# Three streamed weight blocks in two portions: 120 partitions over fifteen DMA engines, 8 over eight

## The chip, the core and the metric

The kernel runs on one core of one Trainium2 chip. The metric is the time of one execution on the device in microseconds; lower is better. The runs shown are three of the kernel before, and one further execution was taken with the hardware profiler.

## The reference

Two independent parts are computed, and their results stand side by side in the last dimension of the output (1, 2048, 2048). Part A is attention over segments with a memory that is carried from one to the next. Its cost lies in a chain of 64 segments, each of which needs the one before:

```python
for s in range(n_seg):                       # 64 segments of 32 rows
    xs = x[:, s * seg_len:(s + 1) * seg_len, :]
    h = jnp.concatenate([mem, xs], axis=1)   # 8 memory rows + 32 rows, 1024 wide
    q = jnp.einsum('btd,dhe->bhte', h, Wq)   # Wq, Wk, Wv: 1024 x 32 heads x 128
    k = jnp.einsum('btd,dhe->bhte', h, Wk)
    v = jnp.einsum('btd,dhe->bhte', h, Wv)
    scores = jnp.einsum('bhqe,bhke->bhqk', q, k) * scale
    p = _softmax(jnp.where(mask[None, None], scores, -1000000000.0), axis=-1)
    o = jnp.einsum('bhqk,bhke->bhqe', p, v)
    o = jnp.einsum('bhte,hed->btd', o, Wo)   # Wo: 32 x 128 x 1024
    mem = o[:, :M, :]
    outs.append(o[:, M:, :])
```

Part B is a state-space convolution of 2048 steps over 1024 channels, done by transforms. It isn't touched by the change.

## The kernel before

**Two stages and a loop.** Part B comes first, together with what of part A does not depend on the chain (the projections of the last 8 rows of each segment, `Ahead`). Then `part_a` runs the chain: a loop of 64 rounds (`for s in range(NS)`, line 406), one per segment, and after it a short end with the output of the rows that were put off (lines 639 to 670).

**The weights.** Wq, Wk, Wv and Wo are cut into 64 blocks of 128 partitions x 2048 bf16 values, 512 KB each, 4096 B per partition. A block of Wk, Wq or Wv has the key (matrix, half of the heads, chunk of the 1024 rows), a block of Wo the key ("o", u). Every round needs all 64. Most of them stay in SBUF for the whole loop, two whole blocks and two halves are kept in other places (`KEPT`, `HALF`), and twelve do not fit: `STREAM` and `STREAM_O` list them, and they are read from DRAM again in every round. In the order of their use within a round these are k02, q02, k11, k15, q14, v02, v07, v14, v17, o4, o8 and o13 (k15 stands for the key ("k", 1, 5) and so on).

**The copies.** The streamed blocks are not read from the inputs but from copies of their own in DRAM. `streamed_copies` (line 63) makes one tile `WD_...` of [128, 2048] for each, with its 128 rows one behind another, and a list of functions, each of which issues one DRAM-to-DRAM transfer on SP's queue (line 69). Part B calls them one at a time between its own work (line 1273).

**The loads.** In the loop `unit(key)` (line 300) hands out a block. For a streamed one it calls `stage` (line 337), which takes the next of four slots (`SLOTS = 4`, tags w0 to w3 of the tile `wst`) in turn and issues one transfer of 128 partitions from the copy, on SP's queue (line 340):

```python
    def stage(key, in_):
        t_ = wst.tile([128, 2048], BF16, name="wst", tag="w%d" % (loads[0] % SLOTS))
        loads[0] += 1
        nc.sync.dma_start(out=..., in_=in_)
        return t_
```

SP issues its transfers in order. Each waits until TensorE has read the block that was in the slot, four blocks earlier, and until the transfers that used this slot and this semaphore before have landed. The first three streamed blocks of the first round are loaded before the loop by `residents` (line 1709). After the loop the three streamed Wo blocks are loaded once more (line 647).

**Other transfers of a round** are issued by ScalarE: the packed left keys `pk` (line 376), the values and rows `vx` (line 382), the store of the left rows (line 392, 128 rows of 512 B) and that of the output rows (line 396, four groups of 32 rows of 512 B).

**The matrix work of a round.** `quads` (line 407) multiplies the 32 rows of the segment with the blocks of one matrix half on TensorE (line 414); its results leave PSUM through ScalarE (line 420). Then come transposes (425), scores (439, 442), the softmax on VectorE and ScalarE, the product with the values (495, 499) and the output projection `oproj` (line 527). Line 627 turns the memory rows back at the end of each round, two transposes, and so marks the rounds in a trace.

Of the kernel before, what the change touches and what calls it, by code (L numbers as in the profile page):

```python
# [10 lines left out]
BF16 = mybir.dt.bfloat16  # L11
# [13 lines left out]

STREAM = {("k", 0): (2,), ("q", 0): (2,), ("k", 1): (1, 5), ("q", 1): (4,), ("v", 0): (2, 7), ("v", 1): (4, 7)}
STREAM_O = (4, 8, 13)

BANK = {("k", 0): "b0", ("q", 0): "b1", ("k", 1): "b2", ("q", 1): "b0", ("v", 0): "b3", ("v", 1): "b2"}
KEPT = {("k", 0, 7): (("K7a", 0, 512), ("K7b", 512, 512), ("K7c", 1024, 512), ("K7d", 1536, 384), (None, 1920, 128)),  # L30
# [28 lines left out]
def streamed_keys():  # L59
    return [key for key in [(m, t, kc) for (m, t), kcs in STREAM.items() for kc in kcs] + [("o", u) for u in STREAM_O]]  # L60


def streamed_copies(ctx, tc, src):
    nc = tc.nc
    dram = ctx.enter_context(tc.tile_pool(name="a_wd", bufs=1, space=bass.MemoryType.DRAM))
    out, copies = {}, []
    for key in streamed_keys():
        t_ = dram.tile([128, 2048], BF16, name="WD_%s" % "_".join(str(i) for i in key))
        copies.append(lambda t_=t_, key=key: nc.sync.dma_start(
            out=t_[:].rearrange("e (h d) -> e h d", h=2) if key[0] == "o" else t_[:], in_=src(key)))  # L70
        out[key] = t_
    return out, copies


class Ahead:
# [3 lines left out]
    def __init__(self, ctx, tc, x, src, seg_len):  # L79
        self.nc, self.tc, self.x, self.src = tc.nc, tc, x, src  # L80
        self.S, self.Dm = x.shape
        self.SL, self.XM = seg_len, 24
        self.XL, self.KC, self.NS = seg_len - 24, self.Dm // 128, self.S // seg_len
        dram = ctx.enter_context(tc.tile_pool(name="a_dram", bufs=1, space=bass.MemoryType.DRAM))
        self.VXd = dram.tile([self.NS + 1, 128, 256 + self.KC * self.XM], BF16, name="VXd")
        self.PKd = dram.tile([self.NS, 128, 512], BF16, name="PKd")
        self.PVd = [dram.tile([self.NS * self.XL, 2048], BF16, name="PVd%d" % t) for t in range(2)]
        self.OLd = dram.tile([self.NS // 8, 128, 8 * 256], BF16, name="OLd")
# [183 lines left out]
def part_a(ctx, tc, x, src, WD, HE, seg_len, out_a, ahead, W_res, rest, places, first):  # L272
    nc = tc.nc
# [26 lines left out]
    def unit(key):  # L300
        if key in rest:

            rest.remove(key)
            load_resident(tc, wres, src, key, W_res, None, places.pop(0)() if places else None)
        if key in W_res:
            return W_res[key]
        if key in KEPT:
            return ahead_of.pop(key) + halves.get(key, [])
        between.pop(key, lambda: None)()
        if key in first:  # L310
            return first.pop(key)
        if key[0] == "v":
            for k_ in rest[0:3 if key[1] == 0 else 1]:
                rest.remove(k_)
                load_resident(tc, wres, src, k_, W_res)
        return stage(key, WD[key][:])

    ctx_l = ctx_w.enter_context(ExitStack())
    pers = ctx_l.enter_context(tc.tile_pool(name="a_pers", bufs=1))
# [14 lines left out]
    def words(out, in_):  # L334
        nc.vector.tensor_scalar(out=out.bitcast(I32), in0=in_.bitcast(I32), scalar1=0, scalar2=None, op0=ALU.bitwise_or)  # L335

    def stage(key, in_):
        t_ = wst.tile([128, 2048], BF16, name="wst", tag="w%d" % (loads[0] % SLOTS))
        loads[0] += 1
        nc.sync.dma_start(out=t_[:].rearrange("e (h d) -> e h d", h=2) if len(in_.shape) == 3 else t_[:], in_=in_)  # L340
        return t_

    def load_kept(key):
# [62 lines left out]
    for s in range(NS):  # L406
# [123 lines left out]
        a = quads("k", 0, (0, 2, 4, 6, 1, 3, 5, 7))  # L530
        k0 = evac(a, "k0")
        a = quads("q", 0, range(0, 6))
# [4 lines left out]
        a = quads("k", 1, range(0, 3))  # L537
# [16 lines left out]
        a = quads("q", 1, range(KC))  # L554
# [3 lines left out]
        a = quads("v", 0, range(0, 3))  # L558
# [34 lines left out]
        a = quads("v", 1, range(0, 5))  # L593
# [46 lines left out]
    wo = {}  # L640
    for u in order:
        if ("o", u) in W_res:
            wo[u] = W_res["o", u]
        else:
            wo[u] = spare.pop(0)
            if ("o", u) in WD:
                nc.sync.dma_start(out=wo[u][:], in_=WD["o", u][:])
            else:
                nc.sync.dma_start(out=wo[u][:].rearrange("e (h d) -> e h d", h=2), in_=src(("o", u)))
    stores(NS - 1, ob)  # L650
# [6 lines left out]
    for b in range(4):  # L657
        pe = [ps_k.tile([128, 512], F32, name="pe", tag="keep%d" % (2 * (b % 2) + n)) for n in range(2)]
        for u in order:
            for hh in range(2):  # L660
                h = 2 * u + hh
                hi = 16 * (h // 16) + 4 * (h % 4) + (h % 16) // 4
# [983 lines left out]
@with_exitstack  # L1646
def kernel(
    ctx: ExitStack,
    tc: tile.TileContext,
    A_x: bass.AP,  # L1650
    A_mem0: bass.AP,
    A_Wq: bass.AP,
    A_Wk: bass.AP,
    A_Wv: bass.AP,
    A_Wo: bass.AP,
    A_seg_len: bass.AP,
    B_u: bass.AP,
    B_A_re: bass.AP,
    B_A_im: bass.AP,
    B_B_re: bass.AP,  # L1660
    B_B_im: bass.AP,
    B_C_re: bass.AP,
    B_C_im: bass.AP,
    B_log_dt: bass.AP,
    B_Dskip: bass.AP,
    out: bass.AP,
):
    seg_len = int(A_seg_len)
    Dm = A_x.shape[2]
    Db = B_u.shape[2]  # L1670
    out_a = out[0, :, 0:Dm]
    out_b = out[0, :, Dm:Dm + Db]
    src = weight_blocks(A_Wq.rearrange("d h e -> d (h e)"), A_Wk.rearrange("d h e -> d (h e)"),
                        A_Wv.rearrange("d h e -> d (h e)"), A_Wo.rearrange("h e d -> (h e) d"))
    WD, copies = streamed_copies(ctx, tc, src)
    ahead = Ahead(ctx, tc, A_x[0], src, seg_len)
    ctx_w = ctx.enter_context(ExitStack())
    W_res, places, first = {}, [], {}
    rest = Keys(RESIDENT)
    rest.ctx = ahead.ctx = ctx_w  # L1680

    def residents(stay, early, uqs, last):
        def put(t_):
            load_resident(tc, None, src, rest.pop(0), W_res, None, t_)
        for _ in range(EARLY[0]):
            load_resident(tc, stay, src, rest.pop(0), W_res)
            yield
        def some(where, tag, n):
            t_ = where.tile([128, n, 2048], BF16, name="W%d" % n, tag=tag)
            return [t_[:, i, :] for i in range(n)]  # L1690
        for t_ in some(stay, "KT1", 2):
            put(t_)
            yield
        for t_ in early:
            put(t_)
            yield
        put(last[0])
        yield
        for t_ in uqs:
            put(t_)  # L1700
            yield
        ahead.wst = ctx_w.enter_context(tc.tile_pool(name="a_wst", bufs=1, side="right"))
        pool = ctx_w.enter_context(tc.tile_pool(name="a_wre0", bufs=1, side="right"))
        for _ in range(EARLY[1]):
            load_resident(tc, pool, src, rest.pop(0), W_res)
            yield
        for i, key in enumerate([("k", 0, 7)] + streamed_keys()[0:SLOTS - 1]):
            first[key] = t_ = ahead.wst.tile([128, 2048], BF16, name="wst", tag="w%d" % i)
            tc.nc.sync.dma_start(out=t_[:], in_=WD[key][:] if key in WD else src(key))
            yield  # L1710
        for i in [c // 2 for c in PAIRS]:
            places.append(lambda i=i: stay.tile([128, 2048], BF16, name="W1", tag="MI%d" % i))
        for i in range(LATE):
            put(places.pop(0)())
            yield
        put(last[1])
        yield

    low = low_blocks(ctx, tc)
    ahead.low = low.pop()  # L1720
    copies += [lambda t_=t_: load_resident(tc, None, src, rest.pop(0), W_res, None, t_) for t_ in low]

    def first_state(m0, xt):
        nc = tc.nc
        consts = constants(tc, ahead)
        hT = next(consts)
        nc.sync.dma_start(out=xt[:].rearrange("p k r -> p (k r)"), in_=ahead.VXd[0, :, 256:])
        nc.sync.dma_start(out=m0, in_=A_mem0[0])
        pm = yield
        for kc in range(8):  # L1730
            nc.tensor.transpose(out=pm[:, kc, :], in_=m0[:, kc * 128:(kc + 1) * 128], identity=ahead.consts[0][0:8, 0:8])
        nc.vector.tensor_copy(out=hT[:, :, ahead.XM:], in_=pm)
        nc.gpsimd.tensor_copy(out=hT[:, :, 0:ahead.XM], in_=xt[:])
        yield
        next(consts)
        yield

    with ExitStack() as ctx_b:
        part_b(ctx_b, tc, B_u[0], B_A_re, B_A_im, B_B_re, B_B_im, B_C_re, B_C_im, B_log_dt, B_Dskip, out_b, ahead, copies, residents, first_state)
    with ExitStack() as ctx_a:  # L1740
        part_a(ctx_a, tc, A_x[0], src, WD, A_Wo.shape[0] * A_Wo.shape[1], seg_len, out_a, ahead, W_res, rest, places, first)
# [35 lines left out]
```

## Time and profile before

| What | us |
|---|---|
| Median of 3 runs | 1962.2 |
| Lowest and highest run | 1956.45 and 1962.97 |
| Span of the profiled execution | 1954.2 |
| TensorE busy in the span | 1810.2 (93%) |
| VectorE busy | 1379.4 (71%) |
| ScalarE busy | 934.7 (48%) |
| GpSimd busy | 443.1 (23%) |
| First and last transpose of line 627 | 649.8 and 1872.3 |

The span goes from the first to the last instruction of the profiled execution; the runs' times include what lies around it. On the page the span is cut into 40 slices of 48.9 us. The loop over the segments begins in the thirteenth of them and ends in the thirty-ninth. Each digit is the busy share of an engine in that slice in tenths. The line of DMA is the mean over the core's 16 DMA engines. In the list of queues q1 is that of SP, q10 that of ScalarE, q0 that of GpSimd, and q8 and q14 carry instructions; the share is the time that their packets took, of 16 engines' span. In the lists of waits a line names who waited and for whom, the sum in us, how often, and the longest.

### The profile page before, as it was taken

Reading aid. Unit: us, or ns where it says so; the run is one execution under the profiler, and the core shown is the slowest. Engines: PE = TensorE matmul, PEld = TensorE weight load, DVE = VectorE, ACT = ScalarE, POOL = GpSimd, SP = SyncE. Lnnn points to the kernel's source line nnn. Section 1 sums busy time; section 2 is a strip of 40 time slices with the busy share of each in tenths; the row PEclk is TensorE's granted clock in tenths of the full one; section 3 lists DMA queues with packets and bytes.
Section 4 is the critical chain, followed back from the end, with each engine's and each line's share of the span. In section 5 each row is a group of like instructions: output and inputs, shape, how many; then the busy total and the mean of one; then the engine's idle time right before and its main releaser. Section 6 shows DMA issues by size and latency. Waiting matters only on the chain.

```text
span 1954.2 us, 74192 instructions
## 1 busy us (share of the span) xinstructions
PE 1810.2 (93%) x31750; PEld 1106.9 (57%) x31788; DVE 1379.4 (71%) x3431; ACT 934.7 (48%) x1670; POOL 443.1 (23%) x855
## 2 busy tenths in 40 slices
PE   8999999887997899999999999999999999998998
PEld 3666666556775555555555555555555555555554
DVE  8599989889994566666676766676766676666650
ACT  8799989851122334344434443444444444444320
POOL 2364545223222111111111111111111111111120
PEclk8999999878998999999999999999999999999999
DMA  7889898867589999999999999999999999999991
GB/s 222 243 232 283 237 287 243 221 188 253 169 272 334 347 340 340 340 339 336 355 339 346 345 335 336 339 341 350 344 350 334 347 341 347 339 350 324 338 343 30
DMA packets 337342, 591.08 MB, mean 302 GB/s; under 512 B 94848, under 2 KB 211048, under 8 KB 334964
## 3 DMA queue, kind: packets, MB, share of 16 engines
q1 hardware_dynamic: 284824, 531.85, 79.9%
q10 hardware_dynamic: 45532, 29.57, 4.9%
q0 software_dynamic: 6656, 24.92, 3.5%
q8 instruction: 249, 4.08, 0.8%
q14 instruction: 81, 0.66, 0.1%
HBM read 528.78 MB, written 68.47 MB: 306 GB/s over the span
## 4 chain that ended last, share of the span: by engine, by line
PE 37%; DMA 27%; DVE 4%; issue 1%; ACT 1%; POOL 0%; SPq 0%; ACTq 0%; DVEq 0%; POOLq 0%
PE acc L414 20%; DMA wst<-WD_v 8%; PE pp L527 8%; DMA wst<-WD_o 7%; DMA wst<-WD_k 3%; DMA arena<-PKd 3%; DMA wst<-WD_q 3%; PE pe L664 3%; PE tr L425 2%; DMA out_dram<-arena 1%; DMA out_dram<-uu 1%; PE pv L495 1%; PE pv L499 1%; DVE arena L621 1%; PE sc L439 1%
## 5 line engine op out<-in xcount | busy, mean ns | idle before, releaser
L414 PEld LDWEIGHTS <-a_hT 128*32 128x32 bf16 x12352 | 328.4, 96 | 324.0 <-issue 64.0
L420 ACT CAST arena<-acc 128x512 bf16<-128x512 f32 x384 | 224.8, 585 | 404.3 <-PE acc L414 324.5
L414 PE MATMUL acc<-wst,a_hT 128*32 128x512 bf16 x2304 | 229.5, 382 | 34.2 <-DMA wst<-WD_v 22.9
L527 PEld LDWEIGHTS <-arena 128*32 128x32 bf16 x8256 | 216.1, 96 | 73.2 <-issue 49.3
L335 DVE TENSOR_SCALAR arena<-keep 128x256 int32<-128x256 int32 (+1 forms) x512 | 175.6, 395 | 28.1 <-PE acc L414 28.0
L428 POOL COPY arena<-arena 128x128 bf16<-128x128 bf16 x128 | 37.3, 292 | 683.0 <-DMA arena<-PKd 314.4
L414 PE MATMUL acc<-XM,a_hT 128*32 128x512 bf16 x2560 | 172.7, 380 | 0.0
L458 ACT ACTIVATE sc<-sc 128x160 f32<-128x160 f32 (+1 forms) x192 | 63.9, 333 | 127.6 <-DVE sc L455 127.6
L454 DVE TENSOR_REDUCE a_mx<-sc 128x4 f32<-128x160 f32 (+1 forms) x192 | 71.7, 374 | 74.7 <-PE sc L442 73.3
L197 PE MATMUL pro<-XM,wsl 128*128 128x512 bf16 x480 | 117.7, 383 | 5.3 <-DVE kst L206 2.2
L527 PE MATMUL pp<-W_o,arena 128*32 128x256 bf16 x3584 | 120.6, 273 | 0.1
L414 PE MATMUL acc<-W,a_hT 128*32 128x512 bf16 x1536 | 120.0, 384 | 0.0
L542 DVE COPY arena<-tr 128x512 bf16<-128x512 bf16 x64 | 27.2, 425 | 128.8 <-PE tr L425 128.8
L462 DVE TENSOR_REDUCE a_mx<-sc 128x4 f32<-128x160 f32 (+1 forms) x192 | 72.9, 379 | 55.3 <-ACT sc L458 54.9
L489 POOL TENSOR_TENSOR arena<-arena,a_BD 128x128 bf16<-128x128 bf16 x128 | 51.1, 399 | 231.1 <-DVE arena L472 229.7
L1266 DVE TENSOR_SCALAR nr<-ptt 128x456 f32<-128x456 int16 x128 | 80.4, 628 | 31.8 <-PE ptt L1244 29.0
L1258 ACT ACTIVATE E<-pa 128x648 bf16<-128x648 f32 x128 | 87.7, 712 | 18.1 <-PE pa L1250 16.0
L414 PE MATMUL acc<-wq,a_hT 128*32 128x512 bf16 x1024 | 92.2, 381 | 0.0
L414 PE MATMUL acc<-g,a_hT 128*32 128x512 bf16 x1024 | 90.4, 379 | 0.0
L1459 POOL TENSOR_TENSOR Bt<-ev 128x512 bf16<-128x512 f32 x32 | 55.7, 1760 | 150.2 <-DVE ev L1456 150.2
L621 ACT CAST arena<-pp 128x128 bf16<-128x128 f32 x64 | 17.0, 265 | 149.8 <-DVE arena L621 149.8
L425 PEld LDWEIGHTS <-arena 128*128 128x128 bf16 x1024 | 57.8, 98 | 54.4 <-issue 45.1
(339 smaller groups left out, 4071.3 us busy)
## 6 DMA issues: line engine op xcount, KB each, us to landing
wst<-WD_v SPq DMA_DIRECT2D x256, 512.0 KB
wst<-WD_k SPq DMA_DIRECT2D x192, 512.0 KB
wst<-WD_o SPq DMA_DIRECT2D x192, 512.0 KB
wst<-WD_q SPq DMA_DIRECT2D x128, 512.0 KB
Ud<-ux POOLq DMA_DIRECT2D x16, 1024.0 KB, 8.2
wq<-Ud SPq DMA_DIRECT2D x32, 512.0 KB
wsl<-in_A_Wk_dram SPq DMA_DIRECT2D x16, 512.0 KB
wsl<-in_A_Wv_dram SPq DMA_DIRECT2D x16, 512.0 KB
```

The costliest lines, as they stand in the source:

```text
L197: nc.tensor.matmul(a[:], lhsT=w[:, kc, 128 * j:128 * j + 128], rhs=xTl[:, kc, :, :].rearrange("p s k -> p (s k)"), start=(kc == 0), stop=( ...
L335: nc.vector.tensor_scalar(out=out.bitcast(I32), in0=in_.bitcast(I32), scalar1=0, scalar2=None, op0=ALU.bitwise_or)
L414: nc.tensor.matmul(a[32 * g:32 * g + 32, o_:o_ + rhs.shape[1]], lhsT=hT[:, kc, :], rhs=rhs, start=(kc == 0), stop=(kc == KC - 1), tile_pos ...
L420: nc.scalar.copy(out=q, in_=a[:])
L425: nc.tensor.transpose(out=p[:, hl, :, :].rearrange("p a b -> p (a b)"), in_=q[:, 128 * hl:128 * hl + 128], identity=ident[:])
L454: nc.vector.tensor_reduce(out=m_, in_=x, axis=AX.X, op=ALU.max)
L458: nc.scalar.activation(out=flat(sc, i), in_=flat(sc, i), func=ACT.Exp, scale=scale)
L462: nc.vector.tensor_reduce(out=m_, in_=x, axis=AX.X, op=ALU.add)
L527: nc.tensor.matmul(po[32 * qt:32 * qt + 32, o_:o_ + rhs.shape[1]], lhsT=oT[:, h % 4, (h % 16) // 4, :], rhs=rhs, start=False, stop=(h == 3 ...
L664: nc.tensor.matmul(pe[n][:], lhsT=left[2 * b + hi // 16][:, 128 * (hi % 16):128 * (hi % 16) + 128], rhs=wo[u][:, 1024 * hh + 512 * n:1024 ...
L1258: sc.activation(out=T["E", r, e // 4][:, lo:lo + 8 * NE].rearrange("p (i c) -> p i c", i=2), in_=T.pop(("p", r, e))[:, :, 0:4 * NE], func= ...
L1266: v.tensor_scalar(out=T["n", r, e // 4][:, lo:lo + 8 * NT], in0=T.pop(("t", r, e))[:, 0:8 * NT].bitcast(I16)[:, 0:16 * NT:2], scalar1=floa ...
```

## The change

Three of the twelve streamed blocks, k15, v07 and o8, get another form; the other nine keep theirs. `PORTIONS` cuts such a block into 120 partitions, dealt to 15 engines, and 8 partitions, dealt to 8. Each portion has a DRAM tile of its own, with one row for each engine: that engine's partitions one behind another (8 x 4096 B, or 1 x 4096 B), and behind them 4096 B that stay unused (`PITCH`), so that the data of one engine begins 36,864 B after the last one's in the large portion, and 8192 B in the small.

A class `Streamed` holds the portions of a block. Its `copy` issues one DRAM-to-DRAM transfer for each portion, and its `load` one transfer into SBUF for each. For the three blocks every copy and every load is thus two transfers on SP's queue where it was one; the tile in SBUF and its four slots are the same. `stage`, the loads after the loop and those before it call `load`. The matrix work is unchanged.

```diff
+PORTIONS = {key: ((120, 15), (8, 8)) for key in (("k", 1, 5), ("v", 0, 7), ("o", 8))}
...
+PITCH = 2048
...
+class Streamed:
+
+    def __init__(self, dram, nc, src, key):
+        self.nc, self.src, self.key, self.pieces = nc, src, key, []
+        lo = 0
+        for i, (rows, engines) in enumerate(PORTIONS.get(key, ((128, 16),))):
+            name = "WD_%s_%d" % ("_".join(str(j) for j in key), i)
+            each = rows // engines
+            if key in PORTIONS:
+                t_ = dram.tile([engines, each * 2048 + PITCH], BF16, name=name)
+                ap = t_[:, 0:each * 2048].rearrange("a (b f) -> a b f", f=2048)
+            else:
+                ap = dram.tile([128, 2048], BF16, name=name)[:]
+            self.pieces.append((lo, lo + rows, ap))
+            lo += rows
+        assert lo == 128
+
+    def copy(self):
+        for lo, hi, ap in self.pieces:
+            flat = ap if len(ap.shape) == 2 else None
+            w = self.src(self.key)[lo:hi]
+            if self.key[0] == "o":
+                w = w.rearrange("(a b) h d -> a b h d", a=ap.shape[0]) if flat is None else w
+                out = ap.rearrange("a b (h d) -> a b h d", h=2) if flat is None else ap.rearrange("e (h d) -> e h d", h=2)
+            else:
+                w = w.rearrange("(a b) f -> a b f", a=ap.shape[0]) if flat is None else w
+                out = ap
+            self.nc.sync.dma_start(out=out, in_=w)
+
+    def load(self, t_):
+        for lo, hi, ap in self.pieces:
+            self.nc.sync.dma_start(out=t_[lo:hi, :], in_=ap)
...
-        t_ = dram.tile([128, 2048], BF16, name="WD_%s" % "_".join(str(i) for i in key))
-        copies.append(lambda t_=t_, key=key: nc.sync.dma_start(
-            out=t_[:].rearrange("e (h d) -> e h d", h=2) if key[0] == "o" else t_[:], in_=src(key)))
-        out[key] = t_
-    return out, copies
+    out = {key: Streamed(dram, tc.nc, src, key) for key in streamed_keys()}
+    return out, [w.copy for w in out.values()]
...
-    def stage(key, in_):
+    def stage(key):
         t_ = wst.tile([128, 2048], BF16, name="wst", tag="w%d" % (loads[0] % SLOTS))
         loads[0] += 1
-        nc.sync.dma_start(out=t_[:].rearrange("e (h d) -> e h d", h=2) if len(in_.shape) == 3 else t_[:], in_=in_)
+        WD[key].load(t_)
         return t_
```

More of the change, by code (lines that the diff above doesn't have):

```diff
@@ L60, in streamed_keys @@
     return [key for key in [(m, t, kc) for (m, t), kcs in STREAM.items() for kc in kcs] + [("o", u) for u in STREAM_O]]
+PITCH = 2048
[28 more added lines that the diff above has]
+            self.nc.sync.dma_start(out=t_[lo:hi, :], in_=ap)
 def streamed_copies(ctx, tc, src):
-    nc = tc.nc
     dram = ctx.enter_context(tc.tile_pool(name="a_wd", bufs=1, space=bass.MemoryType.DRAM))
-    out, copies = {}, []
-    for key in streamed_keys():
-        t_ = dram.tile([128, 2048], BF16, name="WD_%s" % "_".join(str(i) for i in key))
-        copies.append(lambda t_=t_, key=key: nc.sync.dma_start(
-            out=t_[:].rearrange("e (h d) -> e h d", h=2) if key[0] == "o" else t_[:], in_=src(key)))
-        out[key] = t_
-    return out, copies
+    out = {key: Streamed(dram, tc.nc, src, key) for key in streamed_keys()}
+    return out, [w.copy for w in out.values()]
 class Ahead:
@@ L315, in unit @@
                 load_resident(tc, wres, src, k_, W_res)
-        return stage(key, WD[key][:])
+        return stage(key)
     ctx_l = ctx_w.enter_context(ExitStack())
@@ L646, in part_a @@
             if ("o", u) in WD:
-                nc.sync.dma_start(out=wo[u][:], in_=WD["o", u][:])
+                WD["o", u].load(wo[u])
             else:
@@ L1708, in residents @@
             first[key] = t_ = ahead.wst.tile([128, 2048], BF16, name="wst", tag="w%d" % i)
-            tc.nc.sync.dma_start(out=t_[:], in_=WD[key][:] if key in WD else src(key))
+            if key in WD:
+                WD[key].load(t_)
+            else:
+                tc.nc.sync.dma_start(out=t_[:], in_=src(key))
             yield
```

## The prediction

> **What bounds the kernel now.** I read the slices of the span first, then the windows and the transfers of the loop alone, then who waits for whom.
>
> ```profile
> PE   8999999887997899999999999999999999998998
> DMA  7889898867589999999999999999999999999991
> ...
> core 0: us, PE busy (x) PEld busy (x) DVE busy (x) ACT busy (x) POOL busy (x), PEclk, DMA share, GB/s
> 649.80:1872.00 1222.20, 1160.33 (x24863) 676.90 (x24863) 812.64 (x2542) 507.91 (x1117) 192.53 (x496) 1.00 0.96 341
> ```
>
> The loop is where nearly all time lies, and there both TensorE (1160 of 1222 us) and the 16 DMA engines (0.96) are full, at clock 1.00. So the question is which of the two would be shorter alone. The transposes of line 627 come once a round and serve as a clock; the timeline shows the shortest round:
>
> ```profile
> L627 PE MATMUL tro<-a_ident,arena x126: 216/230/231, 649.8 to 1872.3; 128*128 128x128 bf16 x126
> ...
> 1082.29 0.53 PE L627 MATMUL tro<-a_ident,arena 128*128 128x128 bf16 x2
> 1101.19 0.53 PE L627 MATMUL tro<-a_ident,arena 128*128 128x128 bf16 x2
> ```
>
> 63 pairs from 649.8 to 1872.0 make 62 rounds of 19.71 us. The shortest took 18.91 (1082.29 to 1101.19), and six of the 62 lie between 18.91 and 18.96: TensorE's own round. So 0.80 us a round is lost, 50 us in 62 rounds. What TensorE waits for in the loop:
>
> ```profile
> PE acc L414 <- DMA wst<-WD_v: 14.1, 22, 1.1
> PE pp L527 <- DMA wst<-WD_o: 8.5, 17, 1.3
> PE acc L414 <- DMA wst<-WD_k: 6.4, 11, 1.1
> PE acc L414 <- DMA wst<-WD_q: 4.3, 6, 0.9
> ```
>
> These are 33.3 us of waits for streamed blocks; no other waiting of PE in that list is above 4.2. So late loads set the excess. Which DMA engine makes them late? The loop's queues:
>
> ```profile
> q1 hardware_dynamic: 107116, 390.05, 88.4%
> q10 hardware_dynamic: 34968, 23.38, 6.1%
> q8 instruction: 195, 3.19, 1.0%
> ```
>
> The reader sees 195 packets of 16 KB that fetch instructions: 1.0% of 16 x 1222 us is 196 us, so 1.0 us each, 3.15 a round. The run's 4.08 MB of them are 64 B for each of TensorE's 63,538 instructions (matmuls and weight loads of the page), so this is TensorE's own stream. In the trace's packet records no two of the run's 249 fetches overlap, and while one runs the data packets in flight fall from 15.3 to 14.4: one fetch holds one engine. I take it that it is always the same one.
>
> **Work of each engine in a round.** A streamed block gives each engine 8 rows of 4096 B, median 159 ns in the packet records of 1200 to 1500 us: 12 x 8 x 0.159 = 15.26 us. With pk (8 x 46 ns), vx (8 x 41), the left rows' store (8 x 27) and some 15 semaphore packets of 9 ns it is 16.3. The output store (line 396) puts 32 more packets of 27 ns on four engines: 17.2. The engine with the fetches has 16.3 + 3.15 = 19.5, against a round of 19.71: it is full. The mean 4096 B packet takes 180 ns, some 2.0 us a round and engine over the median; the full engine has no room for that, the others have. After idle spells, when sixteen engines start in step, first packets take 200 to 900 ns and later ones 159, so I read this stretch mostly as the price of being ahead. The semaphore increments agree with one straggler: of a load's sixteen, the last comes 0.52 us behind the fifteenth on average, that 0.21 behind the fourteenth, and the gap is 0.79 shortly after a fetch and 0.34 long after one.
>
> **The change part by part.** The sum is made against the profiled execution: its span is 1954.2, the median of the runs 1962.2, so 8.0 lie around it and stay.
>
> 1. Three blocks of twelve pass one engine by: 3 x 8 x 0.159 = 3.8 us a round less on the engine left out. If it is the straggler, 19.5 falls to 15.7. Eight engines take one row more in each: 3 x 0.168 (row and semaphore) = 0.5 us; the four with the output store reach 17.7, still under 18.91. Then TensorE's own round is the bound. What remains over it: the 0.2 us that the round has over the straggler's work today (19.71 - 19.5), which I read as jitter, and 0.1, my estimate, for the four engines that come to 94% of the round. 18.91 + 0.3 = 19.21, 0.50 less than 19.71; over 64 rounds **-32 us**. The ends are -48 (0.75, hardly more than the floor is left) and -17 (0.26, half of the gain given back to jitter).
>
> [...]
>
> 2. Portions 4096 B apart. No row prices this. Its worth lies between nothing and the stretch of three blocks in twelve, 2.0 x 3/12 = 0.5 us a round on engines that aren't the bound. I take 0, as the straggler has little stretch.
>
> 3. Three more DMA instructions a round on SP. They lie between 0.32 us (line 340) and the 0.56 of the four-group store on ACT:
>
> ```profile
> L340 SPq DMA_DIRECT2D wst<-WD_v x256: 319/320/587, 625.9 to 1879.8; - x128
> ...
> L396 ACTq DMA_DIRECT2D out_dram<-arena x63: 547/556/1144, 651.0 to 1873.1; - x63
> ...
> L439 PEldq EVENT_SEMAPHORE  x128: 51/51/51, 627.4 to 1885.1; - x128
> ```
>
> SP issues 12 x 0.32 = 3.8 us in 19.7 and spends the rest in waits for slots, so 1 to 1.7 us more is covered; the eight-row piece queues behind three blocks of 1.27 us. I take 0. Were the cover gone, 0.56 x 3 x 64 = 107 us; the full engines exclude it, as long as loads wait for engines and not for SP.
>
> 4. TensorE waits for two transfers instead of one at three blocks: one semaphore instruction more each, 51 ns (line 439), 3 x 64 x 0.051 = 9.8 us if bare. The scores of line 439 have such an instruction today, and start 0.22 us after the group before where nothing is waited for, as plain groups do. I take 0, with 9.8 as upper end.
>
> 5. SP and ACT share eight semaphores in the trace, and a transfer waits for the one eight back on its semaphore. A round goes from 16 to 19 transfers, so eight back is fewer blocks. SP's loads wait for a slot four blocks back anyway. On ACT the stores (392, 396) and pk, vx (376, 382) can come to wait for a fresh load; queued behind them is the eviction of line 420, and TensorE waits for that. It idles 404 us over 384 of its evictions now, so a few tenths are covered: 0.
>
> 6. Before the loop the three copies (line 69) become six: 3 x 0.6 to 0.95 us of SP between 100 and 320 us, with the loads of lines 121 and 150 behind them; 0 to 2.9, I take 0. The three first loads of line 1709 aren't split blocks; at the end the block o8 of line 647 costs one issue.
>
> Sum: 1954.2 - 32 = 1922 of span, 1962.2 - 32 = **1930 us**.
>
> **The rivals.**
>
> (a) The straggler is one of the eight that take the ninth row, or the fetches aren't on one engine. Its 19.5 lies above the floor of 18.91, so each added ns counts at once: 0.5 us x 64 = 32 us slower, **1994**. Against it for four of the eight: during fetches the output store's packets go on at 81 per us against 78 overall, where a fetch on one of its four engines would leave 58. For it: nothing excludes the next four.
>
> [...]
>
> (b) The straggler is one of the seven between, whose rows don't change: **1962**, the added issues being covered. For it: no row numbers the engine. A relief eaten elsewhere ends at the same place: if the 2.0 us of stretch belongs to the packets and not to being ahead, the four output engines stand at 17.7 + 2.0 = 19.7 and the round stays.
>
> (c) It doesn't do what it says: 120 partitions fall on eight engines of fifteen rows. Then eight engines get 3 x 8 x 0.159 = 3.8 us more: 17.2 + 3.8 = 21.0, 1.3 a round, 83 us slower, **2045**. Against it: narrow transfers in the trace use as many engines as their slowest dimension divides into (four increments for the four-group store).
>
> **How the numbers follow.** That the queue of instructions lies on the engine left out is a judgement: I assume that narrow transfers all begin at the same end; the rows exclude the four engines of that end, and a queue that is kept clear of narrow transfers lies best at the other. I give the forecast 0.65, (a) 0.16, (b) 0.16, (c) 0.03. About 0.3%, 6 us, is what a measurement of this kernel tells from no change. Of the forecast's 0.65 all is faster, of (b) 0.02 too: faster 0.67; the rest of (b), less 0.03 that turn out slower by the costs of 4 to 6, is the same: 0.11; slower 0.16 + 0.03 + 0.03 = 0.22. The forecast's own range is 1914 to 1945 by the ends of part 1. To hold 8 in 10 the range takes in (b) with half of the 9.8 of part 4 and leaves out (a) and (c), 0.19: 1911 to 1968.
>
> **What would show it.** Right: rounds by line 627 near 19.2 with many at 18.9, waits of TensorE for streamed blocks under 15 us, the last increment of an unsplit load closer to the fifteenth, DMA share still above 0.93. Wrong in part 1: rounds at 19.7 (b) or 20.2 (a), with the waits above unchanged or grown. Wrong in 3 to 5: a floor above 19.0, or ACT waiting at lines 392 and 396 with the evictions of line 420 late. Wrong in 2: the mean 4096 B packet falls well below 180 ns.

## The result and the profile after

| | before | after |
|---|---|---|
| Median, us (lowest to highest, 4 runs each) | 1961.12 (1956.45 to 1962.97) | 2181.19 (2178.95 to 2181.40) |
| Span of the profiled execution | 1954.2 | 2179.7 |
| First to last transpose of the loop (line 627, now 659) | 1222.2 | 1439.0 |
| Mean and shortest of the 62 rounds | 19.71 and 18.91 | 23.21 and 21.58 |
| Mean and median 4096 B packet, 1200 to 1500 us, ns | 180 and 159 | 212 and 164 |

The change makes the kernel slower by 220 us: the ratio of the times is 1.113, with a 95% interval of 1.1106 to 1.1152. Of the 225.5 us by which the span grew, 216.8 lie between the first and the last transpose; the loop begins 4.2 us later (654.0 for 649.8) and 4.6 more lie behind it.

These are the slices of the page of the changed kernel, each digit the busy share of a fortieth of the span in tenths:

```profile
PE   8999998879868888788888787888888888888888
...
DMA  7889897675899999999999999999999999999992
```

And this is the loop alone, by the windows:

```profile
core 0: us, PE busy (x) PEld busy (x) DVE busy (x) ACT busy (x) POOL busy (x), PEclk, DMA share, GB/s
653.95:2092.92 1438.97, 1186.20 (x24863) 685.64 (x24863) 810.01 (x2542) 508.62 (x1117) 178.74 (x496) 0.99 0.95 290
```

TensorE does the same matmuls (24,863) in nearly the same busy time (1186 us for 1160), but now in 1439 us, so its digits fall from 9 to 8. The DMA engines are as busy as before (0.95 for 0.96) and yet deliver 290 GB/s instead of 341. It is the same work done more slowly: q1 of the loop moves 390.30 MB in 1439 us, where it moved 390.05 in 1222. The waits of TensorE in the loop are the other half of this:

```profile
PE acc L446 <- DMA wst<-WD_v: 89.4, 98, 2.4
PE pp L559 <- DMA wst<-WD_o: 65.1, 83, 2.1
PE acc L446 <- DMA wst<-WD_k: 49.2, 68, 1.9
PE tro L659 <- DVE arena L653: 9.8, 59, 0.2
```

The first three lines, and q (4.1), make 208 us against 33.3 before: 175 of the 217 us that the loop grew by. The three matrices named are those with a split block each. Where in a round the DMA engines lose their rate is seen when one round is cut into 40 slices. First a round of the changed kernel (1164.8 to 1188.8, slices of 0.60 us), then one of the kernel before (1082.3 to 1101.3, 0.475 us); the upper line of each is the busy share in tenths, the lower the GB/s:

```profile
DMA  9667999999996899979999999899999999999999
GB/s 389 225 178 247 246 250 258 248 266 356 413 392 253 240 316 297 239 164 266 253 382 410 403 416 362 225 225 232 246 218 212 294 430 369 403 396 410 382 348 218
```

```profile
DMA  9999899999999897997999999998989979679979
GB/s 405 379 397 379 328 382 377 370 405 366 368 361 345 303 310 302 391 313 295 360 366 388 379 440 397 397 371 354 388 362 362 328 319 293 224 285 328 345 319 423
```

In the round after there are three troughs, most of their slices at 160 to 270 GB/s under digits that are nearly full (three slices at the head of the first excepted), and 350 to 430 between; before there is none that lasts. Three blocks were changed, and there are three troughs. All rounds together say the same. The packet records, sorted by the time since the last transpose of line 627 (now 659), give the mean 4096 B packet in ns:

```
us into the round      1    3    6   10   11   14   17   18
before               189  178  183  178  176  190  195  177
after                219  273  173  282  270  166  277  286
```

At the troughs 74 to 89% of the 4096 B packets take more than 170 ns, at 7 and 14 us into the round 6 or 7%, as in the loop before as a whole. The 96 such packets that an engine has in a round take 0.032 us more each on average: 3.1 us of the 3.5 that the round grew by. So most of the time went into the packets themselves, in the stretches in which a split block was under way.

### The profile page after: what moved, and what is told of

It reads as the page before. It is cut to its first block, busy times and chain, and to the rows that moved or that the text cites. A ratio compares the mean times of both kernels' runs of the same rounds, so it can differ in the third digit from the quotient of the medians.

```text
span 2179.7 us, 74452 instructions
## 1 busy us (share of the span) xinstructions
PE 1842.8 (85%) x31750; PEld 1118.1 (51%) x31788; DVE 1374.7 (63%) x3431; ACT 935.9 (43%) x1670; POOL 429.9 (20%) x855
## 4 chain that ended last, share of the span: by engine, by line
DMA 51%; PE 17%; DVE 3%; issue 1%; SPq 1%; ACT 0%; ACTq 0%; DVEq 0%; POOL 0%; POOLq 0%
DMA wst<-WD_o 19%; DMA wst<-WD_v 15%; DMA wst<-WD_k 12%; PE pp L559 6%; PE acc L446 6%; PE pe L696 3%; DMA OLd<-arena 2%; DMA out_dram<-arena 1%; DMA out_dram<-uu 1%; DVE arena L653 1%; SPq L98 1%; DVE arena L545 1%; PE tro L659 0%; PE pv L527 0%; DVE arena L497 0%
## 5 line engine op out<-in xcount | busy, mean ns | idle before, releaser
L559 PE MATMUL pp<-wst,arena 128*32 128x256 bf16 x1536 | 78.5, 278 | 91.5 <-DMA wst<-WD_o 65.6
L509 DVE TENSOR_TENSOR arena<-arena,a_BDx 128x512 bf16<-128x512 bf16 x128 | 54.9, 429 | 68.9 <-PE sc L474 56.2
L545 ACT CAST arena<-pv 128x512 bf16<-128x512 f32 (+1 forms) x128 | 61.4, 479 | 78.6 <-DVE arena L545 53.6
```

What stands on the lines that cost most here:

```text
L545: copy(out=o[:, i:i + n], in_=p[:, i:i + n, :].rearrange("p a (g q) -> p a g q", g=4))
L559: nc.tensor.matmul(po[32 * qt:32 * qt + 32, o_:o_ + rhs.shape[1]], lhsT=oT[:, h % 4, (h % 16) // 4, :], rhs=rhs, start=False, stop=(h == 3 ...
```

## The experiments

Each of the twelve was measured once, with one execution of the kernel before on the same chip beside it; 6 us is what such a pair can't tell from no change. Loops are compared with the one trace of the kernel before, which is of another execution. In the expectations H is the theory that the place of the portions in DRAM slows the packets; S that the second transfer of a block, with its issue and its semaphore, does; P that the partitions which each engine writes do, eight consecutive ones for each of the fifteen in the change. How many engines a transfer uses can be counted in its semaphore increments (in the trace of the changed kernel a portion of 8 has eight beside the one that comes at its issue, one of 120 fifteen beside it, an ordinary load sixteen); which partitions an engine writes is in no record, and is the author's inference from the pattern of the transfer.

**e1_pitch0: the portions without the gap.** The changed kernel with its data packed again, all else the same:

```diff
-PITCH = 2048
+PITCH = 0
```

> The changed kernel with the unused 4096 B behind each engine's data taken out (PITCH 0): same portions, same two transfers, data of the engines 32,768 B apart. [...] Theory H (the distance of 36,864 B between portions slows the reads from HBM): back to 1930 to 1975 us, mean packet near 180 ns. Theory S (the second transfer: issue time on SP, and waits on the eight shared semaphores): 2150 to 2210 us with packets as slow as in the changed kernel, as nothing of S is touched.

It took 2182.6 us, rounds of 23.17, 290 GB/s in the loop; the 4096 B packets averaged 216 ns, and the three slow stretches of a round are there at 254, 296 and 289 ns. Its loop by the windows:

```profile
657.00:2093.80 1436.80, 1184.92 (x24862) 687.87 (x24862) 809.36 (x2542) 507.59 (x1116) 178.07 (x496) 0.99 0.99 290
```

The gap of part 2 does nothing that one execution can show, and H, which had 1975 us at the most, is out.

**e2_128over16: one transfer, all sixteen engines, dealt as in the change.** The three blocks are one transfer each again, from a padded copy whose pattern has sixteen engines with eight partitions in a row each:

```diff
-PORTIONS = {key: ((120, 15), (8, 8)) for key in (("k", 1, 5), ("v", 0, 7), ("o", 8))}
+PORTIONS = {key: ((128, 16),) for key in (("k", 1, 5), ("v", 0, 7), ("o", 8))}
```

> The three blocks as one portion of 128 partitions over sixteen engines, portions still 4096 B apart: one transfer a block, 16 transfers a round as before the change, no engine left out. Theory P: the DRAM side's sixteen rows of eight partitions should tie each engine to eight consecutive partitions, so the slow stretches stay: 2050 to 2250 us; if the sixteen engines keep the order of an ordinary 128-partition load, 1950 to 1970. Theory H: 2050 to 2250 us as well. Theory S: 1955 to 1970 us, since the second transfer is gone.

2178.5 us, 2.7 under the changed kernel. There is no second transfer, the round has 16 transfers in the order of the kernel before, and no engine is left out. The loop by the windows, and the round from 1184.4 to 1208.4 in slices of 0.60 us:

```profile
654.60:2090.40 1435.80, 1211.08 (x24862) 701.36 (x24862) 809.67 (x2542) 507.68 (x1117) 175.98 (x496) 0.98 0.97 290
```

```profile
DMA  9879799999999989999999998458999999999997
GB/s 348 307 157 198 210 246 212 242 280 361 391 399 411 308 160 214 270 211 258 264 342 410 396 389 348 184 130 184 266 239 219 239 294 382 396 376 389 396 294 294
```

The same 290 GB/s at a full DMA share, and the same three troughs. This form alone brings the whole loss; S is not needed for it. The slow packets reach TensorE by two ways here: its waits for streamed blocks are 161 us, and it waits 42 us more for ScalarE's evictions, which themselves wait 105 us for the store of the output rows.

**e5_columns: the second transfer without the new dealing.** The kernel before, with the three blocks loaded as two transfers of all 128 partitions, cut across the columns (`CUT` is 1920):

```diff
+        self.cuts = (0, CUT, 2048) if key in PORTIONS else (0, 2048)
...
+        for lo, hi in zip(self.cuts, self.cuts[1:]):
+            self.nc.sync.dma_start(out=t_[:, lo:hi], in_=self.ap[:, lo:hi])
```

> The kernel before, but the three blocks are loaded by two transfers of 128 partitions each, 1920 and 128 columns wide (fifteen sixteenths of the bytes and one): second transfer, SP's issues, TensorE's double waits and the 19 transfers a round as in the change, with ordinary 128-partition loads and ordinary copies. Theory P and theory H: near the kernel before, 1955 to 2010 us (the 128 rows of 256 B cost some 8 x 17 ns an engine and block, 0.4 us a round, about 26 us if they lie on the full engine). Theory S: 2100 to 2200 us.

1958.9 us for 1950.9, 8 more in this one pair. The loop shows none of it: rounds of 19.70, and 1221.6 us from the first to the last transpose for the 1222.2 in the trace of the kernel before. TensorE's waits in the loop:

```profile
PE pp L541 <- DMA wst<-WD_o: 15.5, 25, 2.0
PE acc L428 <- DMA wst<-WD_v: 14.6, 23, 1.4
```

They are 7.0 and 0.5 us above those of the kernel before. Nineteen transfers a round, the longer chain of semaphores and TensorE's double wait, all as in the change, cost the loop nothing that shows. With e2 this separates the cause: the second transfer without the new dealing is all but free, the new dealing without the second transfer costs everything.

**e6_three_forms: is it the partitions, or the pattern in DRAM?** e1 and e2 share with the change a copy that is read with three dimensions (engine, row, column). Here only v07 has it:

```diff
+PORTIONS = {("k", 1, 5): (64, 64), ("v", 0, 7): (32, 32, 32, 32), ("o", 8): (32, 32, 32, 32)}
+PADDED = ("v", 0, 7)
...
+                t_ = dram.tile([8, 5 * 2048], BF16, name="%s_%d" % (name, i))
+                self.pieces.append((32 * i, 32 * i + 32, t_[:, 0:4 * 2048].rearrange("a (b f) -> a b f", f=2048)))
```

> The three blocks arrive in three different ways in one kernel, all with 128 rows. Block k15: two transfers of 64 partitions from an ordinary copy, sixteen engines with four partitions each. Block o8: four of 32 from an ordinary copy, sixteen engines with two each. Block v07: four of 32 from a copy of eight padded portions, so eight engines with four each, the pattern in DRAM with three dimensions as in the changed kernel. Twenty-four transfers a round, so waits on transfers may add; only the packets in the three windows are compared.
> [...]
> Rival theory T (the three-dimensional pattern in DRAM slows the packets): k15 and o8 stay at 160 to 200 ns, v07 alone is slow, at 250 ns and more.
> [...]

2285.2 us, with 23 transfers a round in the trace where the expectation counted 24; the whole time isn't compared. The mean 4096 B packet in the slowest us of each window: k15, with two-dimensional patterns, 287 ns, 90% of them above 170; o8, the same, 293 and 86%; v07, the only one with three dimensions, 260 and 67%, and its five us run 166, 182, 219, 260 and 217. Theory T has it the wrong way round and falls. P is left. v07 is the mildest, about 210 on average, quick at first and slow later. Its four transfers read four DRAM tiles of one and the same pattern, so that what differs between the quick and the slow ones is the partitions they write (and what else is then under way).

How the partitions come to slow the packets is not shown: no record here names the engine of a packet. The trace of the changed kernel shows the price, 273 to 286 ns at the troughs' centres against 159, the median of an ordinary packet, a factor of 1.7 to 1.8, only while such a load is under way.

**z1_only_o8: the price of one block.** The changed kernel with only o8 split, seventeen transfers a round:

```diff
-PORTIONS = {key: ((120, 15), (8, 8)) for key in (("k", 1, 5), ("v", 0, 7), ("o", 8))}
+PORTIONS = {key: ((120, 15), (8, 8)) for key in (("o", 8),)}
```

> The changed kernel with only block o8 as 120 + 8 partitions; k15 and v07 load as before, seventeen transfers a round, and the transfer eight behind pk is v17 as in the kernel before. Theory P says the price belongs to each split block by itself: one slow window a round instead of three (4096 B packets at 250 ns or more there, under 200 elsewhere), and 50 to 90 us over the kernel before, since a third of the 220 us is 73; less if the slot in front of o8 has slack. Rival theory C (the loss comes from the three together, by a queue that never gets ahead again, or from the waits behind pk that the order of nineteen transfers brings): under 20 us.

2049.3 us for 1959.9: 89 more, at the upper edge of what P gave, and C falls. Rounds take 21.14. The round from 1162.3 to 1182.3 in slices of 0.50 us:

```profile
DMA  9989999999997679989999999978999999999999
GB/s 344 303 303 360 393 336 320 328 397 376 402 363 289 254 295 383 357 311 361 333 385 385 369 401 401 361 229 287 262 295 188 221 205 229 361 401 418 401 410 385
```

One long trough is left, from 13 to 17 us, where o8 is loaded, with mean packets of 280 to 285 ns over all rounds; the two others are gone. Each split block carries its own price.

**e4_extra8: the semaphores that transfers share.** The kernel before, with one more transfer behind each of the three loads, eight rows of the copy to a scratch buffer in DRAM that nothing reads:

```diff
+        if key in EXTRA:
+            nc.sync.dma_start(out=spill[EXTRA.index(key)][:], in_=in_[0:8])
```

> The kernel before, and behind each load of the three blocks one more transfer on SP of eight rows of 4096 B from the same copy into a scratch tile in DRAM, which nobody reads: one row more for eight engines, 19 transfers a round, no engine relieved, loads unchanged. Theory P and H: 1955 to 1975 us if the engine that fetches instructions is not one of the eight, 1985 to 2005 if it is. Theory S: 2050 to 2200 us, from the waits on shared semaphores alone.

The eight rows did not go as eight packets of 4096 B: between 1200 and 1500 us the records hold 688 packets of 2048 B, sixteen for each transfer, or three in a round for each engine if all sixteen take the same share, so this tests mainly the number and order of transfers. It cost 72 us (2022.5 for 1950.9), between the 2005 that P and H had at the most and the 2050 that S had at the least, with packets at 159 in the median and 183 in the mean. Three packets of 84 ns (their median) are 0.25 us a round, so the added work itself can be up to 16 of the 72 us, if the engines had no room for it. SP's queue waits for the transfer of pk:

```profile
SPq L343 <- DMA arena<-PKd: 134.0, 62, 3.5
```

In the order of issue the transfer eight behind pk was block v17 before, which SP issues long after pk has landed (in the loop of the kernel before it waits for pk 0.4 us in all). Here it is v07, and SP, held there, issues nothing behind it. The changed kernel has the same order and the same wait:

```profile
SPq L98 <- DMA arena<-PKd: 198.7, 62, 4.5
...
SPq L98 <- DMA out_dram<-arena: 54.2, 46, 2.2
```

S thus has a real mechanism. But e2 has pk ahead of v17 and next to none of this wait (1.9 us), and is only 2.7 us faster: behind the slow packets the wait adds next to nothing. In e5 it is the short second piece of v07 that stands eight behind pk, and SP waits for pk 23 us in all.

**The dummies: would the relief have been worth anything?** The prediction rested on one full engine, the sixteenth. A transfer added each round, DRAM to DRAM with six rows for each of its engines, asks which engines are full. First behind o13, here for sixteen engines (90 and 15, 48 and 8 in the other two):

```diff
+        if key == ("o", 13):
+            nc.sync.dma_start(out=spill, in_=in_[0:96].rearrange("(a b) f -> a b f", a=16))
```

> The kernel before, with one transfer more a round, behind the load of block o13: DRAM to DRAM, fifteen engines with six rows of 4096 B each, into a scratch buffer that nothing reads. It asks which engine is the one that the prediction called the straggler (19.5 us of work in a round of 19.71), and whether there is one. Six rows more at 159 ns are 0.95 us a round, 61 us over 64 rounds, for an engine that is full; an engine with 16.3 us takes them into its idle time.
> Theory L (the full engine is the sixteenth, the one that the change left out): x15 costs under 15 us, x16 45 us or more, x8 under 15 us.
> Theory F (it is one of the first eight): all three cost 45 us or more. Theory M (one of 8 to 14): x15 and x16 do, x8 does not.
> Theory N (there is no such engine; the fetches go over many): all three cost under 20 us, with rounds near the 18.91 us of the matmuls plus what the loads fall behind. Theory A (all sixteen are full): x16 about 60, x15 about 57, x8 about 30.

> As x15_dummy with sixteen engines of six rows each. L, F, M: 45 us or more; N: under 20; A: about 60.

> As x15_dummy with eight engines of six rows each. F: 45 us or more; L, M, N: under 15 to 20; A: about 30.

Against 1953.4 they took 2077.6, 2087.1 and 2067.3: 124, 134 and 114 us more. No theory gave this; more than 100 us don't depend on the engines at all. The waits of SP in x16:

```profile
SPq L342 <- DMA arena<-PKd: 242.9, 62, 5.1
```

It is e4's wait again: the extra transfer moved pk ahead of v02. These three don't answer the question. With the dummy behind v17 the order of the other transfers stays, and no wait of SP for pk is left in y16:

```diff
-        if key == ("o", 13):
+        if key == ("v", 1, 7):
```

> The question of x16_dummy again, with the dummy transfer (DRAM to DRAM, sixteen engines with six rows of 4096 B) behind the load of block v17 instead of o13. The three x kernels cost 114 to 134 us, nearly alike for eight, fifteen and sixteen engines, with 238 to 247 us of SP's queue waiting for the transfer of pk in front of block v02: the added transfer had moved pk eight transfers ahead of v02. Here the order of all other transfers is that of the kernel before, and the one eight behind pk is v17 again, so that this wait should be gone and only the work of the engines is left.
> Theories as for x15_dummy. L (the full engine is the sixteenth), M (one of 8 to 14), F (one of the first eight): 45 us or more. N (no such engine): under 20 us. A (all sixteen full): about 60.

> As y16_dummy with fifteen engines of six rows. L: under 15 us, that is 30 us or more below y16; F, M: within 10 us of y16 and 45 or more; N: under 20; A: about 57.

> As y16_dummy with eight engines of six rows. F: 45 us or more, as y16; L, M: under 15 us; N: under 20; A: about 30.

Against 1959.4: y16 48 us more, y15 53, y8 18. The loops of y16, y15 and y8 by the windows:

```profile
652.00:1923.60 1271.60, 1160.90 (x24862) 678.70 (x24862) 811.94 (x2542) 508.55 (x1116) 189.21 (x496) 1.00 0.97 347
```

```profile
652.40:1927.70 1275.30, 1159.91 (x24863) 675.70 (x24863) 811.76 (x2542) 508.57 (x1117) 191.37 (x496) 1.00 0.96 345
```

```profile
651.20:1893.40 1242.20, 1162.79 (x24863) 678.25 (x24863) 812.91 (x2542) 508.12 (x1117) 192.85 (x496) 1.00 0.96 346
```

Leaving out one engine saves nothing. If it is the one that the change left out, as the author takes it (no record numbers them), L falls: that engine does not set the end. F would have y8 as dear as y16, and N all three under 20; both fall. y8 lies between M (under 15) and A (about 30). Whether all sixteen are about equally full or some of 8 to 14 more than the rest stays open. For M speaks the shortest round: 19.53 and 19.54 us in y16 and y15, but 18.90 in y8, as in the kernel before. For A speaks that y16 and y15 move 347 and 345 GB/s, hardly more than the 341 of the kernel before, at the same 0.96 of the DMA share: what was added had to be paid for with 0.80 and 0.86 us a round, of 0.95 that six rows take. A third reading is open too. TensorE's waits in y16 grew where the loads straight behind the dummy are used, and hardly elsewhere:

```profile
PE pp L531 <- DMA wst<-WD_o: 72.8, 81, 3.1
PE acc L418 <- DMA wst<-WD_v: 16.7, 30, 1.5
```

Wo had 8.5 and Wv 14.1 in the kernel before. The price may thus be that of loads which come just in time at this one place, and not of engines that are full all round.

The dummies also answer for the reading side. By its pattern each engine of y16's dummy reads six rows in a row of a copy, as the engines of a split block read eight, but writes them to DRAM. Between the landing of block v17 and that of the dummy the 4096 B packets take 164 ns on average, and 3% of them more than 170. Reading a block in this division is not slow by itself; with the quarters of v07 in e6 this leaves the side that is written, the SBUF.

## Why the prediction was wrong

**What bounds the kernel.** Right that the loop is near both limits and that late loads set the excess. Wrong that the engine which the change leaves out sets it: by y15, if it leaves out the same one, rows on the fifteen others cost as much as rows on all sixteen (53 us and 48). That the fetches lie on this engine, and that narrow transfers all begin at the same end, were the author's assumptions; no run shows them. Whether another single engine does, or all sixteen, stays open. The work of an engine was put together from median packets, and the 2.0 us of stretch a round were read "as the price of being ahead", so the others seemed to have 2.5 to 3.4 us of room. At least some of them had hardly any where the dummy stood: 0.95 us of rows cost 0.80 to 0.86. The DMA share of 0.96 in the loop leaves an engine 0.8 us of idle time a round on average.

**Part 1 failed, and decided.** It priced the rows of a split block at the 159 ns of an ordinary load and counted only how many rows an engine has, not which partitions they go to. While a split block is loaded, the 4096 B packets take 270 to 290 ns at the centres of the troughs. e2 shows this price without any engine left out, e5 its absence with everything else in place, z1 one block's share of it. The -32 us and both ends of that term were sized on the wrong duration; the loop grew by 217. Even the gain on the other side has nothing behind it: by y15, read in the same way, the engine that is left out isn't the one that holds the round. Nor did its sign come: the last increment of an unsplit load still comes 0.54 us behind the fifteenth, where the prediction read 0.52 before. No rival of the prediction let a packet take longer by the partitions that it goes to, and so the range ended at 1968.

**Part 2** (the gap, 0): right; e1 differs by 1.4 us, within what one execution can't tell.

**Part 3** (issue on SP, 0): the cover held, the bounds didn't. The median issue of the 120 partitions takes 0.87 us and that of the 8 partitions 0.47, beside 0.32 for an ordinary load: 1.02 us more for each block, 3.1 a round, where 1 to 1.7 was said. In e2, with one issue of 0.52 for such a block, the time is the same.

**Part 4** (the double wait, 0): right. e5 has it at the same three blocks, and its loop is as long as before.

**Part 5** (shared semaphores, 0): its sum held only by luck. It expected SP's loads to be unaffected and ScalarE's transfers to wait. ScalarE did: its evictions wait 90 us for transfers in the loop, where it was 6. But so did SP, 199 us for pk. In kernels whose packets are quick SP's wait costs most of the 72 us of e4 and, with the dummies behind o13, 71 to 96 us more than the same dummies cost behind v17 (x16 134, y16 48). The step counted how many blocks eight transfers are, and not which late transfer would stand eight ahead of which load.

**Part 6** (copies before the loop, 0 to 2.9): the loop starts 4.2 us later, a little above the end. This can't be put down to the copies: in x8 and e5, whose copies are the ordinary ones, it starts 5.3 and 3.7 us later.

**The rivals.** (a) and (c) are not what happened: by y8, if its eight engines are those that take the ninth row, these don't set the end (18 us for rows on them, 48 on all sixteen), and the increments count fifteen engines for the 120 partitions, not eight. (b) would have left the time where it was, had the packets stayed at their price, and both its halves are still open: that the straggler is one of the engines between (theory M), and that the stretch belongs to the packets and eats the relief (theory A). The signs named for a wrong part 1 (waits grown, rounds at 20.2) came, with three times the excess. The sign named for part 2 was one-sided: it looked only for shorter packets, and they got longer.

## What to carry over

Before a load is cut by partitions, or given another split over engines, ask for each engine which partitions it writes, not only how many rows: here 128 partitions in the ordinary form took 159 ns a packet, and every other division by partitions that was tried (120 + 8, sixteen times 8 in a row, two times 64, four times 32) took 260 to 296 at its worst; a cut by columns cost the loop nothing. Don't take the time that a DMA share of 0.96 hides in long packets for room: six more rows for every engine, 0.95 us, cost 0.80 of it. When the number of transfers in a loop changes, write down which transfer stands eight behind each late one: a load that waits there holds every load behind it (SP waited 199 us for pk in the changed kernel, 243 in x16).

## What was not expected of the hardware

The transfers with the new division slowed others that were under way as well: the 1024 B packets of pk, untouched by the change, rose from 46 to 61 ns in the median (1200 to 1500 us), and stay at 46 in z1, where no split block comes near them. And one more transfer a round that nothing reads cost 114 to 134 us in one place and 18 to 53 in another: here the order in which transfers take their semaphores (243 us of waits for pk in x16, none in y16) was worth more than the rows that they move.
